# Chunks 4 and 5 of an mLSTM in 64x64 tiles, and FFN2 of the first group ahead of FFN1 of the third

## The chip, the cores and the metric

The kernel runs on one NeuronCore of a Trainium2 chip. The core has a matrix engine (TensorE, PE in the profile; its weight loads are PEld), three engines for elementwise work (VectorE or DVE, ScalarE or ACT, GpSimd or POOL), and a queue (SyncE, SP) that mostly issues DMA transfers; POOL issues some too. Each engine works through its own instructions in the order in which they were written, and waits on semaphores for the others. The metric is the device time of one execution in microseconds (us).

## The reference

An mLSTM cell runs over 4 batches, 8 heads and 768 time steps with 40 numbers per head; its output, as rows of 320, goes through a feed-forward network with a squared ReLU. Everything is in 32-bit floats; the two weight matrices arrive as 64-bit floats.

```python
for t in range(S):
    kt, vt, qt = (k[:, :, t], v[:, :, t], q[:, :, t])
    m_new = np.maximum(f_gate[:, :, t] + m, i_gate[:, :, t])
    f_stab = np.exp(f_gate[:, :, t] + m - m_new)
    i_stab = np.exp(i_gate[:, :, t] - m_new)
    m = m_new
    C = f_stab[:, :, None, None] * C + i_stab[:, :, None, None] * np.einsum('bhd,bhe->bhde', vt, kt)
    n = f_stab[:, :, None] * n + i_stab[:, :, None] * kt
    h_tilde = np.einsum('bhde,bhe->bhd', C, qt)
    denom = np.maximum(np.abs(np.einsum('bhd,bhd->bh', n, qt)[:, :, None]), 1.0)
    y[:, :, t] = h_tilde / denom / (1.0 + np.exp(-o_gate[:, :, t]))
x = y.transpose(0, 2, 1, 3).reshape(3072, 320)
out = np.maximum(x @ w_in, 0.0) ** 2 @ w_out        # w_in 320 x 2048, w_out 2048 x 320
```

## The kernel before

**Chunks and groups.** Time is cut into 24 chunks of 128 steps (`NT`), six per batch (`NB`). Within a chunk the recurrence becomes products of matrices: scores (keys by queries), scores times a matrix W of decays, that times the values (the numerators), and a state C carried to the next chunk of the batch. Two chunks make a group (`GT`), 12 groups in all; FFN1 and FFN2 work on a group's 256 rows. Chunks and groups are numbered from 0.

**Two forms of a chunk.** Chunks 0 to 5 (below `X_SQ`) use the whole 128x128 array: `transposes` turns keys and queries, `scores` multiplies them, `weigh` makes W with one exponential per head, `weighted` applies it, and `attend` computes `hi` (old state by queries, L622), `dC` (new state, L634) and `hp` (values by weighted scores, L645). `normalise` divides on DVE, `turn_rows` turns the rows of x for the FFN on PE (L848, L850), and ACT copies them out (L853).

Chunks from 6 on use 64x64 quarters of the array. `attend_begin` and `attend_end` hold two halves of the products into `numT`: `values_of_C` (old state, L708), `values_of_P` (values, L727), `new_C` (new state, L738). Between the halves stands one tiny DVE instruction (L700) that reads the last result of the first half, and the second half waits for it. The numerators come out turned. DVE transposes 32x32 squares of them (`tn`, L758); `store_num` writes them to memory, `load_num` reads them back in another order, `normalise_turned` divides, `store_rows` and `load_rows` take x through memory the same way, and `turn_squares` (L840) finishes the turning. `decays` (L488, L492) gives the old state's factors, which `scale_q` (L672) puts on the queries; `decay_C` scales the old state on POOL. From chunk 7 on (`KQ_SQ`) keys and queries are turned in the same manner (`pair_up`, `load_squares`, `turn_kq`), from chunk 8 on (`ROT`) the causal zeros are skipped too.

**Weights.** `Rounding` brings the 64-bit weights in 18 pieces: `fetch` loads one on SP (L210), `words` makes two conversions on ACT (L220, L222), `join` three instructions on DVE (L231 to L236) and one on POOL (L240), after which it fetches the next. Pieces 0 to 9 are `w_in`, 10 to 17 `w_out`.

**FFN.** Groups 0 and 1 have a plain FFN1 (`ffn1`, L874 and L885; `relu_half` and `square_half` on ACT), group 0 a plain FFN2 (`ffn2`, L911, 64 products). From group 2 (FFN1) and group 1 (FFN2) on, seven products of half-size blocks do the work of eight. FFN1 then is `ffn1_open`, `ffn1_rows` (64-row products, L1090) and `ffn1_close`, whose sums end on DVE at L1111; it needs sums of weights (`sums_of_win`) and of x (`sums_of_x`, on DVE for group 2, else on POOL). FFN2 is `ffn2_fast` in four steps (L965), with sums of weights (`sums_of_weights`, T0 to T2 and B12 in place) and of activations (`sums`, S1 to S4).

**Order.** It is written out by hand. After a set-up that ends at about 25 us, a first loop of eight passes (u) does chunks 2 to 5, two passes each, beside FFN1 of groups 0 and 1, while pieces of weights arrive. A second loop (n) runs over quarters of FFN work: four parts for FFN1 of group 2, four for FFN2 of group 0, then FFN2 of group g and FFN1 of group g + 2 in turn. Chunk 6 + n // 4 runs beside them: its scores and `weighted` in its first part, `attend_begin` and `attend_end` in its second, the next chunk's weighing and its own normalising in its third. Loads of keys and values (`load`) go out on SP below chunk 10 and on POOL from there. `NEXT` and `LAST` say how many pieces of weights are joined after each pass or part.

PSUM has eight banks. In the first loop three are for FFN1 (`ps_h`), two for others (`ps_o`) and three for attention (`ps_at`); in the second loop five and three. A product that wants a bank waits until the earlier result has been copied out of it.

Of the kernel before, what the change touches and what calls it, by code (L numbers as in the profile page):

```python
# [29 lines left out]
def kernel(  # L30
# [80 lines left out]
    bdm = conv.tile([P, PR, 2, D1], F32, bufs=1)  # L111
# [13 lines left out]
    def make_consts():  # L125
# [24 lines left out]
        nc.gpsimd.memset(bdm[:], 1.0)  # L150
        nc.gpsimd.memset(bdm[:DP, :, 1, :], 0.0)
        nc.gpsimd.memset(bdm[DP:, :, 0, :], 0.0)
# [30 lines left out]
    class Rounding:  # L183
# [41 lines left out]
        def join(self):  # L225
# [16 lines left out]
            if n != LENT - 1:  # L242
                self.fetch()
# [95 lines left out]
    KQ_SQ, X_SQ, ROT = 7, 6, 8  # L339
# [22 lines left out]
    def load_k(s):  # L362
        (dst, src), _, _ = load_parts(s)
        b, c = divmod(s, NB)
        src = src[b, :, c * P : (c + 1) * P, :].rearrange("h p d -> p h d")
        eng = nc.sync if s < 10 else nc.gpsimd
        eng.dma_start(dst[:, :PR], src[:, :PR])
        for n in range(2):
            eng.dma_start(dst[HALVES[n], PR:], src[HALVES[1 - n], PR:])

    def load_v(s):
# [3 lines left out]
        eng = nc.sync if s < 10 else nc.gpsimd  # L375
# [15 lines left out]
    def kqT(s):  # L391
        t = kqT_b[s % NKT]
        st[s]["kT"], st[s]["qT"] = t[:, 0], t[:, 1]
        return t
# [69 lines left out]

    def mask(s):
# [14 lines left out]
    def decays(s):  # L480

        if s % NB > 0:
            e = st[s]["eA"] = kq_b[2 + s % 2][:, 1].rearrange("p (j two) d -> p j (two d)", two=2)
# [10 lines left out]
    def weigh(s, masked=False, part=None, vw=True):  # L494
# [4 lines left out]
        if s < X_SQ and part != 1:  # L499
# [8 lines left out]
        for i in (range(len(A) if s < ROT else 0) if part is None else (part,)):  # L508
# [5 lines left out]
            if s < X_SQ:  # L514
# [84 lines left out]
    C_old = []  # L599

    def decay_old(s):
        if s + 1 < NB:
            Cd = st[s]["Cd"] = old.tile([P, PR, 2, D1], F32, name="Cd", bufs=1)
            nc.gpsimd.tensor_tensor(
                Cd[:].rearrange("p j i d -> p (j i) d"), C_old[(s - 1) % 2][:].rearrange("p j i d -> p (j i) d"),
# [3 lines left out]
    def attend(s):  # L609
# [41 lines left out]
        if c > 0:  # L651
            num = d["num"] = old.tile([P, H, D1], F32, name="num", bufs=1)
            nc.vector.tensor_tensor(
                num[:], hi[:], eA_T[:, b, c, :].unsqueeze(2).to_broadcast([P, H, D1]), op=ALU.mult,
# [3 lines left out]
        if c + 1 < NB:  # L658
            Cn = C_old[s % 2]
            if c == 0:  # L660
                nc.vector.tensor_tensor(Cn[:], dC[:], bdm[:], op=ALU.mult)
# [12 lines left out]
    def decay_C(s):  # L674
        if s % NB > 0:
            Cd = st[s]["Cd"] = attn.tile([P, PR, D1], F32, name="Cd", bufs=1)
            nc.gpsimd.tensor_tensor(
                Cd[:], C_b[(s - 1) % 2][:, : PR * D1].rearrange("p (j d) -> p j d", d=D1),
# [3 lines left out]
    LIVE = [slice(DP * i, DP * i + D) for i in range(2)]  # L682

    def attend_begin(s):
# [13 lines left out]
        else:  # L698
            end, spare = out[1][DP : DP + 1, P : P + 1], C_b[(s - 1) % 2][0:1, 4 * D1 : 4 * D1 + 1]
        nc.vector.tensor_scalar(spare, end, scalar1=0.0, scalar2=None, op0=ALU.mult)  # L700

    def values_of_C(s, rows, order=(0, 1)):
        d = st[s]
        C = C_b[(s - 1) % 2]
        for e in order:
            for m in order:
                i, j = rows[m], 2 * m + e
                nc.tensor.matmul(  # L708
                    d["numT"][m][HALVES[e], i, :], lhsT=C[LIVE[i], j * D1 : j * D1 + DP], rhs=d["eA"][LIVE[i], j, :],
# [33 lines left out]
    def attend_end(s):  # L743
# [11 lines left out]
        tn = attn.tile([P, P // SQ, PR, SQ], F32, name="tn", bufs=1)  # L755
        to = tn[:].rearrange("p m c r -> p c m r")
# [3 lines left out]
        if c + 1 < NB:  # L760
            Cn = C_b[s % 2][:, : PR * D1].rearrange("p (m x) -> p m x", m=2)
            for m in range(2):
                dC = d["out"][m][:, 2 * P : 2 * P + 2 * D1]
                if c > 0:
                    nc.vector.tensor_tensor(
                        Cn[:, m], dC, d["Cd"][:].rearrange("p (m e) d -> p m (e d)", m=2)[:, m], op=ALU.add,
# [5 lines left out]
    def store_num(s):  # L772
        nc.sync.dma_start(n_d[s], st[s]["tn"][:].rearrange("p m j r -> p (m j r)"))

    def load_num(s):
        N = st[s]["N"] = kq_b[s % 2][:, 1].rearrange("p h d -> p (h d)")
# [28 lines left out]
    def normalise(s):  # L805
        d = st[s]
        num = d["num"]
        if num is not d["hp"]:
            nc.vector.tensor_tensor(num[:], num[:], d["hp"][:], op=ALU.add)
# [96 lines left out]
    def ffn2(g, j, part):  # L906
        if part == 0:
            st["o_ps"] = ps_h.tile([P, W], F32, name="h_ps")[:, :DM]
        o_ps = st["o_ps"]
        for fb in range(part * NF // 2, (part + 1) * NF // 2):  # L910
            nc.tensor.matmul(  # L911
                o_ps, lhsT=st["g2", g][:, fb, j * P : (j + 1) * P], rhs=w_out[:, fb, :],
                start=(fb == 0), stop=(fb == NF - 1),
            )
        if part == 1:
            y = ffn.tile([P, DM], F32, name="y_sb", bufs=3)
            nc.scalar.copy(y[:], o_ps)
            t = g * GT + j
            nc.sync.dma_start(out[t * P : (t + 1) * P, :], y[:])

# [118 lines left out]
    def ffn1_begin(g):  # L1046
        new_g2(g)
        xT = st["xT", g]
        begun = st["begun"] = [
            (ps_h.tile([P, 4, P], F32, name="h_ps"), ffn.tile([P, 4, P], F32, name="r_sb", bufs=4)) for _ in range(2)  # L1050
        ]
        for q, (X, m1) in enumerate(begun):
            blocks(X, F11, xT[:, 0, 0, :], q, True)
            nc.scalar.copy(m1[:], X[:])
        for q, (X, m1) in enumerate(begun):
            blocks(X, F12, xT[:, 0, 1, :], q, False)

    def ffn1_open(g, q):
        if q == 0 and g > 2:
            new_g2(g)  # L1060
        xT, xs = st["xT", g], st["xs"]
        begun = st["begun"].pop(0) if g == 2 else None
        X = begun[0] if begun else ps_h.tile([P, 4, P], F32, name="h_ps")
        Y, V, Z = [ps_h.tile([P, 4, P], F32, name="h_ps") for _ in range(3)]
        st["f1"] = X, Y, V, Z
        m1 = begun[1] if begun else ffn.tile([P, 4, P], F32, name="r_sb", bufs=4)
        U2, U4 = [ffn.tile([P, 4, P], F32, name="r_sb", bufs=4) for _ in range(2)]
        st["U"] = U2, U4
        if not begun:
# [391 lines left out]
```

## Time and profile before

| | us |
|---|---|
| median of the three runs | 492.54 (490.52 to 492.83) |
| the profiled execution, in all | 491.22 |
| its span in the profile | 489.4 |
| PE busy | 481.7 |
| DVE busy | 341.8 |
| ACT busy | 240.4 |
| POOL busy | 215.3 |

The profile records one execution. For each instruction it gives its engine, the line of the program, its start and duration, and what released it when the engine had been idle before. A 32-bit product appears as two instructions (so "x16" is eight products), and a matmul's own duration overlaps the next one's; the chain of work shows what each group adds to the time. Rows of the chain are: start, length, engine and line, count. Rows of a timeline are: start, length, engine, line, operation, output<-input, shapes, count, and in brackets idle time before it and its releaser. Stage rows give, for a stretch, its length and each engine's busy time with the number of its instructions, the granted clock of TensorE, and the busy share of the DMA engines. Waits are: who, for whom, total, times, longest.

### The profile page before, as it was taken

What the parts mean: (1) busy time and instruction counts of PE and PEld (TensorE: products, weight loads), DVE (VectorE), ACT (ScalarE), POOL (GpSimd) and SP (SyncE); (2) the same over time, 40 slices, a digit from 0 to 9 for tenths busy, and PEclk for the clock granted to TensorE, in tenths of its full rate; (3) what the DMA queues carried; (4) which work ended last, traced back from release to release, by engine and by line L of the source; (5) the groups of instructions that cost most, each with busy time, mean ns of one, the idle gap of its engine ahead of it and who ended that gap; (6) DMA issues with size and microseconds to landing.
All of it is one profiled execution on the core that took longest, in us unless ns stands there. A gap on an engine that the chain in (4) does not pass through costs nothing.

```text
span 489.4 us, 15237 instructions
## 1 busy us (share of the span) xinstructions
PE 481.7 (98%) x6169; PEld 449.0 (92%) x6169; DVE 341.8 (70%) x704; ACT 240.4 (49%) x531; POOL 215.3 (44%) x322
## 2 busy tenths in 40 slices
PE   9999999999999999999999999999999999999997
PEld 4886788897799999999999999999999999999996
DVE  7799767888946856957966956857856956635441
ACT  4676996764522650942742941742942640513300
POOL 6455533432679178078179078078174040020000
PEclk9999999999999999999999999999999999999999
DMA  9999997745878579758759778658665612200000
GB/s 185 227 243 227 304 230 183 151 84 140 171 130 199 120 138 225 134 107 212 135 99 219 140 117 208 134 109 213 123 106 129 149 51 82 55 28 2 3 27 29
DMA packets 191096, 68.08 MB, mean 139 GB/s; under 512 B 158833, under 2 KB 180241, under 8 KB 191025
## 3 DMA queue, kind: packets, MB, share of 16 engines
q1 hardware_dynamic: 185280, 57.50, 55.1%
q0 software_dynamic: 5600, 9.50, 8.1%
q8 instruction: 49, 0.80, 0.7%
q14 instruction: 23, 0.18, 0.1%
q10 hardware_dynamic: 144, 0.10, 0.1%
HBM read 54.77 MB, written 18.01 MB: 149 GB/s over the span
## 4 chain that ended last, share of the span: by engine, by line
PE 87%; ACT 5%; SPq 4%; DMA 3%; issue 1%; DVE 0%; ACTq 0%
PE h_ps L965 35%; PE h_ps L1041 26%; PE h_ps L1090 8%; PE h_ps L911 4%; PE h_ps L874 3%; PE numT L727 3%; PE numT L708 2%; DMA lent_t<-in_moe_w_in_dram 1%; PE numT L738 1%; SPq L210 1%; PE tp L575 1%; PE h_ps L575 1%; SPq L1151 1%; ACT g_c L511 1%; DMA raw<-in_moe_w_in_dram 1%; DMA og<-in_o_gate_dram 1%
## 5 line engine op out<-in xcount | busy, mean ns | idle before, releaser
L475 POOL TENSOR_SCALAR_AFFINE_SELECT A_bc<-A_bc 64x512 f32<-64x512 f32 x32 | 22.5, 704 | 80.4 <-ACT kq L492 57.9
L965 PE MATMUL h_ps<-T,S 128*128 128x160 f32 x352 | 51.7, 300 | 0.6 <-ACT g_c L1107 0.6
L1071 ACT COPY r_sb<-h_ps 128x512 f32<-128x512 f32 x18 | 10.5, 585 | 84.2 <-PE h_ps L1041 84.2
L965 PEld LDWEIGHTS h_ps<-T,S 128*128 128x128 f32 x352 | 48.9, 190 | 1.1 <-ACT g_c L1107 0.9
L965 PE MATMUL h_ps<-w_out,g 128*128 128x160 f32 x336 | 49.2, 303 | 0.0
L981 DVE TENSOR_TENSOR y_sb<-y_sb,h_ps 128x160 f32<-128x160 f32 x44 | 14.1, 320 | 47.7 <-PE h_ps L965 47.6
L965 PEld LDWEIGHTS h_ps<-w_out,g 128*128 128x128 f32 x336 | 46.1, 190 | 1.3 <-issue 0.5
L1041 PE MATMUL h_ps<-xT,w_in 128*128 128x128 f32 x320 | 42.8, 278 | 0.0
L1041 PE MATMUL h_ps<-lent_t,w_in 128*128 128x128 f32 x320 | 42.2, 275 | 0.0
L1041 PEld LDWEIGHTS h_ps<-xT,w_in 128*128 128x128 f32 x320 | 38.9, 192 | 1.4 <-issue 1.0
L1090 PE MATMUL h_ps<-xT,w_in 64*64 64x128 f32 x960 | 39.1, 272 | 0.0
L1041 PEld LDWEIGHTS h_ps<-lent_t,w_in 128*128 128x128 f32 x320 | 38.9, 192 | 0.2 <-issue 0.2
L1041 PE MATMUL h_ps<-lent_t 128*128 128x128 f32 x320 | 39.0, 275 | 0.0
L1041 PEld LDWEIGHTS h_ps<-lent_t 128*128 128x128 f32 x320 | 37.3, 192 | 0.0
L505 ACT ACTIVATE A_bc<-A_bc,b_R 128x64 f32<-128x64 f32 (+1 forms) x128 | 35.7, 361 | 1.8 <-POOL A_bc L475 1.4
L1090 PEld LDWEIGHTS h_ps<-xT,w_in 64*64 64x64 f32 x960 | 34.8, 133 | 1.3
L379 POOL DMA_DIRECT2D va<-in_v_dram x56 | 34.2, 619 | 1.8 <-DMA kq_rows<-in_q_dram 1.3
L758 DVE STREAM_TRANSPOSE tn<-numT 128x256 f32<-128x256 f32 x36 | 14.0, 428 | 28.5 <-PE numT L708 19.2
L874 PE MATMUL h_ps<-xT,w_in 128*128 128x256 f32 x128 | 30.1, 385 | 1.6 <-ACT xT L853 1.2
L874 PEld LDWEIGHTS h_ps<-xT,w_in 128*128 128x128 f32 x128 | 23.4, 190 | 6.1 <-POOL w_in L240 1.6
L1033 POOL TENSOR_TENSOR lent_t<-xT 128x128 f32<-128x128 f32 (+1 forms) x18 | 14.6, 833 | 32.7 <-DVE xT L840 32.7
L965 PE MATMUL h_ps<-w_out,g_c 128*128 128x160 f32 x192 | 28.0, 302 | 0.0
(218 smaller groups left out, 1150.0 us busy)
## 6 DMA issues: line engine op xcount, KB each, us to landing
A_bc<-a_slots SPq DMA_DIRECT2D x32, 256.0 KB, 4.4
num_rows<-tn SPq DMA_DIRECT2D x18, 256.0 KB, 2.3
kq<-num_rows SPq DMA_DIRECT2D x72, 64.0 KB, 2.1
raw<-in_moe_w_out_dram SPq DMA_DIRECT2D x7, 640.0 KB, 5.4
kqT<-kq_rows SPq DMA_DIRECT2D x34, 128.0 KB, 3.3
og<-in_o_gate_dram SPq DMA_DIRECT2D x24, 160.0 KB, 4.9
out_dram<-y_sb SPq DMA_DIRECT2D x24, 160.0 KB, 3.1
raw<-in_moe_w_in_dram SPq DMA_DIRECT2D x7, 512.0 KB, 6.9
```

The source lines that it names most:

```text
L379: eng.dma_start(dst[HALVES[n], PR * (1 - late_keys) : PR * (2 - late_keys)], src[HALVES[late_keys], PR * m : PR * (m + 1)],)
L475: nc.gpsimd.affine_select(part, part, compare_op=ALU.is_ge, fill=-1e30, base=0, pattern=[[0, PR], [0, 2], [1, DP]], channel_multiplier=-1,)
L505: nc.scalar.activation(A[0][:, x, to], A[0][:, x, to], AF.Exp, bias=b_R[:, b, c, own, x : x + 1],)
L727: nc.tensor.matmul(d["numT"][m][HALVES[e], i, t0:], lhsT=va_w[s % NKQ][keys, at * D1 : at * D1 + DP], rhs=rhs, start=(s % NB == 0 and i == ...
L758: nc.vector.transpose(to[:, 2 * m : 2 * m + 2], d["numT"][m].rearrange("p c t -> p (c t)"))
L874: nc.tensor.matmul(hs[i][:, n, :], lhsT=w_in[:, a, fb * P : (fb + 1) * P], rhs=xT[:, :, a, :], start=(n == 0 and a == 0), stop=False,)
L911: nc.tensor.matmul(o_ps, lhsT=st["g2", g][:, fb, j * P : (j + 1) * P], rhs=w_out[:, fb, :], start=(fb == 0), stop=(fb == NF - 1),)
L965: nc.tensor.matmul(to, lhsT=lhsT[:, p], rhs=rhs[:, p, :], start=(start and p == 0), stop=(p == NPAIR - 1), skip_group_check=True,)
L981: add = lambda to, a, b: nc.vector.tensor_tensor(to, a, b, op=ALU.add)
L1033: sub = lambda to, a, b: eng.tensor_tensor(to, a, b, op=ALU.subtract)
L1041: nc.tensor.matmul(to[:, n, :], lhsT=lhsT[:, 4 * q + n, :], rhs=rhs, start=(start and n == 0), stop=True, skip_group_check=True,)
L1090: nc.tensor.matmul(to[cols, n, :], lhsT=w_in2[rows, 4 * q + n, cols], rhs=rhs, start=(start and n == 0), stop=True, skip_group_check=True,)
```

## The change

`X_SQ` goes from 6 to 4, so chunks 4 and 5 take the quarter form. Their `decays` and `scale_q` are new work in the first loop; their numerators and rows go through memory; their og gets the second ACT copy of `half_tanh`. Chunk 4's old state is still in the layout of the whole-tile form, so `values_of_C` picks its columns out of it. W for chunks 4 and 5 is masked after the exponential (`mask_W`) and not before. In u = 2 chunk 4's exponentials move ahead of a piece's `words`. The block mask `bdm` goes: two copies onto a zeroed tile take its place.

In the second loop FFN2 of group 0 is first and FFN1 of group 2 second; FFN2's products run in an order that needs the last piece of `w_out` only in the fourth part; `ffn1_begin`, a split opening for group 2, goes. The sums move to other parts: sums of weights 0, 1, 3, 2 to n = 3, 4, 9, 9 (they were 0, 1, 2, 3 at n = 5, 6, 7, 8), S1 and S2 of group 1 to n = 6 and 7 (both were at n = 6). Chunks 8 and 9 are loaded at n = 5 and 6 on POOL (they were loaded in u = 5 and u = 7 on SP), chunk 10 at n = 8; og for 8 and 9 comes at n = 3, `pair_up` for 8 and 9 at n = 0 and 2. Chunk 7's numerators are stored (n = 5) before chunk 6's rows are loaded back.

```diff
@@ set-up @@
-    bdm = conv.tile([P, PR, 2, D1], F32, bufs=1)
...
-        nc.gpsimd.memset(bdm[:], 1.0)
-        nc.gpsimd.memset(bdm[:DP, :, 1, :], 0.0)
-        nc.gpsimd.memset(bdm[DP:, :, 0, :], 0.0)
...
-    KQ_SQ, X_SQ, ROT = 7, 6, 8
+    KQ_SQ, X_SQ, ROT = 7, 4, 8
...
-        eng = nc.sync if s < 10 else nc.gpsimd
+        eng = nc.gpsimd
...
+    def mask_W(s):
+        nc.gpsimd.affine_select(
+            st[s]["W"], st[s]["W"], compare_op=ALU.is_ge, fill=0.0, base=0, pattern=[[0, H], [1, P]],
+            channel_multiplier=-1,
+        )
@@ decay_old, attend, values_of_C @@
+            if s >= X_SQ:
...
+                for i, rows in enumerate(HALVES):
+                    nc.gpsimd.tensor_tensor(
+                        Cd[rows], C_old[(s - 1) % 2][rows, :, i, :],
+                        st[s]["dec"][rows, i::2].unsqueeze(2).to_broadcast([DP, PR, D1]), op=ALU.mult,
+                    )
+                return
...
-            if c == 0:
-                nc.vector.tensor_tensor(Cn[:], dC[:], bdm[:], op=ALU.mult)
+            for i in range(2 if c == 0 else 0):
+                nc.vector.tensor_copy(Cn[HALVES[i], :, i, :], dC[HALVES[i], :, i, :])
...
+    def state(s):
+        return (C_b if s >= NB else C_flat)[s % 2]
...
+                at = (2 * j + i if s == X_SQ else j) * D1
@@ ffn2 @@
+    F2 = [(j, fb) for half in ((0, 8), (8, 14), (14, 16)) for j in range(GT) for fb in range(*half)]
+
+    def ffn2(step):
+        if step == 0:
+            st["o_ps"] = [ps_h.tile([P, W], F32, name="h_ps")[:, :DM] for _ in range(GT)]
+        for j, fb in F2[8 * step : 8 * step + 8]:
...
+        if step == 3:
+            for j, o_ps in enumerate(st["o_ps"]):
+                y = ffn.tile([P, DM], F32, name="y_sb", bufs=3)
+                nc.scalar.copy(y[:], o_ps)
+                nc.sync.dma_start(out[j * P : (j + 1) * P, :], y[:])
@@ first loop @@
-    WIN_SUMS = {5: 0, 6: 1, 7: 3}
+    WIN_SUMS = {5: (0, 1), 6: (3,)}
...
             if u == 2:
+                weigh(4, masked=True, vw=False)
+                decays(4)
                 rounding.words()
             weighted(s)
...
             if u == 2:
-                mask(s + 1)
                 rounding.join()
+                mask_W(4)
                 rounding.join()
-                weigh(s + 1, masked=True)
+                values(4)
                 rounding.words()
             else:
...
-                weigh(s + 1, masked=(u == 0), vw=(u > 0))
+                weigh(s + 1, masked=(u != 6), vw=(u == 6))
+                if u == 4:
+                    mask_W(5)
                 square_half()
+                if u > 0:
+                    scale_q(s)
...
-            attend(s)
+            if s < X_SQ:
+                attend(s)
+            else:
+                attend_begin(s)
+                attend_end(s)
+                store_num(s)
...
-            for r in {5: (8,), 7: (9,)}.get(u, ()):
-                load(r)
-            for r in {5: (7,), 7: (8,)}.get(u, ()):
-                pair_up(r)
+            if u == 5:
+                pair_up(7)
+            if u == 7:
+                load_A(7)
             if u > 4:
-                load_o(2 * s)
-                load_o(2 * s + 1)
+                load_num(s)
             transposes(s + 1, (True, True))
             rounding.words()
             ffn1(u // 4, u % 4)
             square_half()
+            if u == 5:
+                decays(5)
+            if u == 7:
+                normalise_turned(4)
+                store_rows(4)
+                rounding.fetch()
+                rounding.join()
...
+        if u == 6:
+            load_squares(7)
...
-    turn_rows(5)
-    load_squares(7)
@@ second loop @@
-    parts = [(1, 2, i) for i in range(4)] + [(2, 0, i) for i in range(4)]
-    for g in range(1, NG):
+    parts = []
+    for g in range(NG):
...
+        if n == 0:
+            turn_kq(7)
+            pair_up(8)
+            load_rows(4)
+            rounding.words()
+            rounding.join()
...
             do(store_num, s)
+            if n == 1:
+                normalise_turned(5)
+                store_rows(5)
+                turn_squares(4)
+            if n == 5:
+                load_rows(6)
             do(load_num, s)
+            if n == 1:
+                load_rows(5)
+                weigh(7, masked=True)
+                sums_of_win(2)
             do(load_squares, s + 2)
...
-        if 5 <= n < 8:
-            sums_of_weights(n - 5)
-        if n == 6:
-            sums(1, slice(0, NPAIR), (1, 2))
+        if n == 3:
+            load_o(8)
+            load_o(9)
+            sums_of_weights(0)
         if n == 8:
-            sums_of_weights(3)
             sums(1, slice(0, NPAIR), (3,))
         if n == 9:
+            sums_of_weights(3)
             sums(1, slice(0, NPAIR), (4,))
+            sums_of_weights(2)
...
-        if n == 0:
-            ffn1_begin(g)
-            sums_of_x(g)
-            sums_of_win(2)
...
+            if n == 6:
+                sums(1, slice(0, NPAIR), (1,))
+                turn_squares(6)
...
+            if n == 2:
+                pair_up(9)
+                turn_squares(5)
+                sums_of_x(2)
...
+        if n in (5, 6):
+            load(3 + n)
+            load_o(5 + n)
+        if n == 8:
+            load(10)
...
+        if n == 4:
+            sums_of_weights(1)
+        if n == 7:
+            sums(1, slice(0, NPAIR), (2,))
```

## The prediction, made before the changed kernel was run

> **What bounds the kernel now.** I read the page's busy shares first, then the busy time by stage, then the waits of PE, then the chain of work around the edited stages, and last the timelines of ACT and DVE there. Chunks are numbered from 0, as in the code, so the change concerns chunks 4 and 5; u counts the eight passes of the first loop, n the parts of the second.
>
> ```profile
> span 489.4 us, 15237 instructions
> PE 481.7 (98%) x6169; PEld 449.0 (92%) x6169; DVE 341.8 (70%) x704; ACT 240.4 (49%) x531; POOL 215.3 (44%) x322
> ```
> ```profile
> 59.00:91.06 32.06, 30.90 (x221) 25.51 (x217) 23.37 (x38) 27.01 (x55) 11.85 (x9) 1.00 0.93 196
> 91.06:130.09 39.03, 38.75 (x485) 32.25 (x488) 33.41 (x66) 23.42 (x51) 15.82 (x23) 1.00 0.60 124
> ```
> ```profile
> PE h_ps L874 <- ACT xT L853: 1.2, 1, 1.2
> ```
>
> From 60.56 us on TensorE pauses hardly at all (0.28 in the second stage), at a granted clock of 1.00. So this time is a sum of TensorE's work, and a change is worth the products it takes away, less the pauses it brings. The stage lines (length, then busy PE, PEld, DVE, ACT, POOL, clock, DMA share) show what stands close behind: ACT with 27.01 of 32.06 us in the stage of chunks 4 and 5, DVE with 33.41 of 39.03 us in the next. The one long wait of PE is for the copy of chunk 3's rows, behind a full ACT queue.
>
> ```profile
> 65.35 1.05 PE hi L622 x8
> 66.40 0.89 PE dC L634 x8
> 67.29 1.75 PE hp L645 x16
> ...
> 74.47 0.37 PE tp L848 x2
> 74.83 0.37 PE tp L850 x4
> ```
> ```profile
> 114.54 0.38 PE numT L708 x8
> 114.92 0.44 PE numT L727 x16
> 115.36 0.26 PE numT L738 x16
> ...
> 115.64 0.17 DVE kq L700
> ...
> 115.85 0.44 PE numT L738 x16
> 116.29 0.46 PE numT L727 x16
> 116.75 0.22 PE numT L708 x8
> ```
> ```profile
> 48.93 0.68 ACT L220 ACTIVATE mag<-raw 128x512 f32<-128x512 f32 x1 [4.27 <-DMA raw<-in_moe_w_in_dram]
> 50.08 2.43 ACT L511 ACTIVATE g_c<-A_bc,b_T 128x128 f32<-128x128 f32 x8
> ```
> ```profile
> 169.12 0.68 DVE L1111 TENSOR_TENSOR g<-r_sb,h_ps 128x512 f32<-128x512 f32 x1
> ```
>
> The first of these is chunk 4 in whole tiles, the second chunk 7 in quarters: the two prices that the change trades.
>
> **Part 1, chunk 4 in quarters.** Goes: hi, dC and hp, 1.05 + 0.89 + 1.75 = 3.69, and the turning of its rows, 0.37 + 0.37 = 0.74. Comes: chunk 7's row, 114.54 to 116.97 = 2.43, since chunk 4 too has a state before and after, works below ROT and has nothing between the halves. Gain 1.26 + 0.74 = 2.00.
>
> **Part 2, chunk 5.** Goes: 1.05 + 1.75 = 2.80 (no state follows) and 0.74. Comes: 0.38 + 0.44 in the first half, the wait for L700 (115.61 to 115.85, 0.24) with the refilling behind it (0.44 instead of the 0.21 of the same products at 155.30, so 0.23), then 0.22 + 0.46: 1.97. Gain 0.83 + 0.74 = 1.57.
>
> [...]
>
> **Part 3, ACT at u = 2.** The exponentials of chunk 4 (2.43) and its decays (2 of 0.62) go ahead of a weight piece's two conversions. ACT idles 4.27 us there, from 44.65 to 48.93, so they fit: 44.65 + 2.43 + 1.25 = 48.33. After it ACT no longer has the 2.43 at 50.08. The next piece (issued at 45.28) lands at 51.29, so ACT runs 52.52 - 51.3 = 1.2 us earlier through the relu, square and copies up to L853. Of PE's 1.16 us of wait I take 1.10 as gone; bounds 0 and 1.16.
>
> **Part 4, FFN2 of group 0 ahead of FFN1 of group 2.** The number of products is the same. Chunk 7's halves now stand around the 64-row products, as chunk 9's do at 152.50 (0.38, 0.44, 0.21, then 0.21, 0.46, 0.22 = 1.92), and not bare: 2.43 - 1.92 = 0.51. FFN1 of group 2 loses its split opening: 6.50 + 6.45 = 12.95 against 3.57 + 9.13 = 12.70 for group 3, 0.25. Gain 0.76, bounds 0 and 0.76.
>
> Gains: 2.00 + 1.57 + 1.10 + 0.76 = 5.43. The new clock, for what follows: chunk 6's scores (89.97 before) start at 89.97 - 4.67 = 85.3, FFN2 of group 0 at 86.4, chunk 6's halves at 86.4 + 4.5 = 90.9; with chunk 7's scores they take 1.48 + 0.88, to 93.3; the other 13.12 of FFN2 end at 106.4, the first part of FFN1 at 110.0 (3.57), chunk 7 with the 64-row products between its halves (1.92 + 1.77) at 113.7, its state on DVE (0.78 + 0.35) at 114.9.
>
> **Part 5, what DVE gets late.** S2 of group 1 was made at n = 6, far ahead; now it stands at n = 7 behind the closing sums of FFN1. In group 3 these ended at 169.72, 2.70 after PE had gone on to the scores at 167.02. With S2's 1.22 that is 3.92; PE wants S2 after scores (0.67) and half of a step (4.54 / 2), 2.94. So PE waits 1.0; bounds 0 and 1.5. The fourth sum of weights (1.48) moves from n = 8 to behind chunk 8's state at n = 9: state done 138.91, so 140.39, against 137.87 + 2.27 = 140.14 for the product that reads it: 0.3 with the semaphore; bounds 0 and 0.5. The other moved sums (weights 0, 1, 2, S1, S3, S4, the first two of w_in) stand behind work that PE does not want next.
>
> **Part 6, POOL.** Loads of chunks 8 and 9, seven issues each, move from SP to POOL and from u = 5, 7 to n = 5, 6: 14 x 0.62 = 8.7 us. They come behind Cd(8), which needs chunk 7's state (114.9). Then: Cd 0.5, load(8) 4.5, waiting for its last landing 2.4 to 5.8, vw 0.75, pair_up(10) 2.1, load(9) 4.5, load(10) 4.5, mask(9) 1.4, Cd(9) 0.5, load(11) 4.5, spreading 1.8, vw(9) 0.75, the sums of x for group 3 1.6. With 3.8 of waiting this ends at 146.2; PE wants them at 132.4 (end of chunk 8, 137.87 less 5.43) + 11.06 + 0.89 + 1.3 (part 5) = 145.7. I take 0.5; bounds 0 (landing in 2.4) and 2.5. DVE's weighting of chunk 9 waits behind vw(9), with the closing of FFN2 behind it.
>
> [...]
>
> **Costs set at nothing.** ACT gains 2.5 of decays and 0.94 of copies of og and loses two row copies of 0.48: from 64.3 it then runs without a gap until 79.4, and the tightest relu is 0.7 ahead of the bank that PE wants at u = 6; without that, each us is a us. SP: two chunks more of storing and loading (0.34 + 1.75 + 0.38 + 1.85, 4.3 each) take the place of the two loads (4.5 each); two og loads and their issues go to n = 3. Two waits stand in SP's queue: chunk 4's rows wait for its normalising (1.9 on DVE in u = 7), and behind them the last raw piece, which FFN2 reads at about 104.5; chunk 5's rows wait for its normalising, and behind them chunk 6's numerators (landing by 101, normalised from 101.8 on, when DVE is through with weights and chunk 7), chunk 5's rows, chunk 8's squares (wanted at 118) and decays (110). DVE: L700, tn, state and normalising (0.16 + 0.78 + 0.35 + 1.9) with scale and turn (0.7 + 0.55) are 4.4, as the old row (4.4 from 66.44). The x of chunk 5 must reach FFN1 of group 2: normalised by 96.4 (tn and state of chunk 6 to 94.5, then 1.9), stored in 3.5 (as at 109.66), loaded in 3.5 (as at 113.24) to 103.4, turned behind chunk 6's normalising and summed by 105.6; PE wants it 0.89 after 106.4, at 107.3: cover 1.7. The set-up (a second zeroing of 0.4 on POOL, three less, two copies for one product on DVE, 0.2 more) lies beside the first loads.
>
> **Sum.** -5.43 + 1.0 + 0.3 + 0.5 = -3.63. The profiled execution had 489.4 of span and 491.22 in all: 487.6. It lies 1.3 under the median of 492.54; between 487.6 and 488.9 I say 488.3.
>
> **Rivals.** (a) The gain is given back: the next piece lands late so the 1.10 stays, and POOL is 2.5 late: -5.43 + 1.10 + 1.3 + 2.5 = -0.5, 490.7. For it: POOL's chain has no slack; against: the landing at 51.29 is on record. (b) No new wait shows, since DVE is ahead at n = 7 and POOL's landings are short: -5.43, 485.8. Against it: the closing sums can't start before PE has finished the part. (c) Slower: the x of chunk 5 comes late to n = 4. Each us beyond the 1.7 of cover costs one; it decides from 5.3 us late. For it: at 130.87 the same load took 6.95, twice the 3.5. With both hops doubled it is loaded at 110.4 and summed at 112.1, a pause of 4.8; with that alone added, -3.63 + 4.8 = +1.2, 492.4. Against it: no POOL loads run at that time in the new order.
>
> **How the numbers follow.** Mine 0.45, (a) 0.25, (b) 0.12, (c) and what is like it 0.18. Half a per cent, 2.5 us, is about what a measurement can tell. Mine is beyond it nine times in ten, (b) always, (a) seldom: faster 0.55, same 0.27, slower 0.18. The range goes from (b), 485.8 less some scatter, to (c), 492.4 with the median's 1.3: 485.0 to 494.0; mine alone is 486.5 to 490.5.
>
> **What would show it.** No hi, hp or tp L848 after 60 us; quarters of 2.4 and 2.0 us for chunks 4 and 5; no wait of PE for L853; FFN2 of group 0 starting near 86; a wait of 1 us for DVE's S2 near 128; POOL without idle time from 115 to 146. I am wrong if PE waits between 100 and 110 for the sums of x, or in the first loop for relu.

## The result, and the profile after

Over twelve executions each, the changed kernel and the kernel before have the same median, 492.24 us (490.80 to 495.06 against 490.52 to 492.83): a ratio of 1.0006, 95% interval 0.9989 to 1.0024. I had forecast 488.3, 4.2 us under the median that I then knew. The profiled execution took 491.6, with this head of its page:

```profile
span 489.9 us, 15406 instructions
PE 477.5 (97%) x6229; PEld 445.9 (91%) x6229; DVE 343.4 (70%) x719; ACT 242.9 (50%) x534; POOL 228.3 (47%) x335
```

TensorE has 4.2 us less to do (481.7 before) and needs 0.5 more of span: its idle time went from 7.7 to 12.4 us. So the products were saved, and pauses took the time back. Where, the busy time by stage tells (length of the stretch, then busy PE, PEld, DVE, ACT, POOL, granted clock, DMA share, GB/s). After the change the stretches are: to the scores of chunk 6 and the start of FFN2; to the scores of chunk 8 (n = 8); to FFN1 of group 3 (n = 12); to its second block of products; the rest.

```profile
60.51:87.61 27.10, 26.22 (x273) 21.54 (x273) 20.81 (x41) 24.82 (x51) 12.31 (x7) 1.00 0.93 209
87.61:125.76 38.15, 38.15 (x480) 32.22 (x484) 30.89 (x69) 18.79 (x43) 18.48 (x24) 1.00 0.73 157
125.76:148.40 22.64, 19.21 (x265) 18.35 (x258) 17.31 (x26) 10.52 (x26) 20.55 (x31) 1.00 0.98 164
148.40:150.22 1.82, 1.05 (x10) 0.86 (x8) 1.47 (x4) 0.59 (x1) 1.77 (x4) 1.00 0.92 232
150.22:489.90 339.68, 335.94 (x4792) 328.66 (x4792) 222.86 (x479) 144.34 (x311) 143.92 (x223) 1.00 0.54 117
```

The kernel before, in the stretch that answers to the third (it runs 0.13 us into FFN1 of group 3, which starts there at 148.77):

```profile
130.02:148.90 18.88, 18.88 (x259) 18.47 (x259) 11.76 (x22) 4.58 (x15) 13.26 (x21) 1.00 0.82 145
```

Chunk 8's scores start at 125.76 instead of 130.02, 4.26 us sooner; that much of the 5.43 was made. In the third stretch PE idles 3.4 of 22.64 us where it had idled none, and another 0.8 in the fourth. From the second block of FFN1's products on, both kernels need 339.7 us. The same products of the third stretch also keep PE busy for 19.21 us instead of 18.75 (to 148.77). I put this down to the last product ahead of a pause, which overlaps no next one: the five instructions ahead of the longest pause, in the timeline below, took 0.95 us, 0.19 each, and the 27 behind it 3.94, 0.15 each. The waits of PE name three pauses for that stretch (us in total, times, longest):

```profile
PE h_ps L980 <- issue: 2.2, 1, 2.2
PE h_ps L980 <- DVE S L975: 1.2, 1, 1.2
...
PE h_ps L1056 <- POOL lent_t L1051: 0.8, 1, 0.8
PE h_ps L896 <- ACT xT L875: 0.7, 1, 0.7
```

The first three are 4.2 us and take back all but 0.06 of the 4.26; with the 0.46 more of busy time the span is 0.5 longer than before. The timeline of PE (start, duration, and in brackets the idle time ahead and who ended it) shows all three. In the longest, of the 16 instructions of a step of L980, five ran and then nothing for 2.24 us, though no semaphore was waited for ("issue"):

```profile
130.17 2.41 PE L980 MATMUL h_ps<-T,S 128*128 128x160 f32 x16 [1.19 <-DVE S L975]
...
134.92 0.95 PE L980 MATMUL h_ps<-w_out,g 128*128 128x160 f32 x5
138.11 3.94 PE L980 MATMUL h_ps<-w_out,g 128*128 128x160 f32 x27 [2.24 <-issue]
...
148.40 1.05 PE L1056 MATMUL h_ps<-xT,w_in 128*128 128x128 f32 x8
150.22 2.05 PE L1056 MATMUL h_ps<-lent_t 128*128 128x128 f32 x16 [0.77 <-POOL lent_t L1051]
```

POOL explains the wait of 0.77. After the change its timeline reads:

```profile
133.53 0.62 POOL L365 DMA_DIRECT2D kq<-in_k_dram  x1 [0.77 <-DMA kq<-in_k_dram]
134.60 0.62 POOL L375 DMA_DIRECT2D va<-in_v_dram  x1 [0.45 <-DMA kq<-in_k_dram]
135.51 0.62 POOL L375 DMA_DIRECT2D va<-in_v_dram  x1 [0.29 <-DMA va<-in_v_dram]
136.54 1.22 POOL L375 DMA_DIRECT2D va<-in_v_dram  x2 [0.41 <-DMA va<-in_v_dram]
137.77 2.29 POOL L478 TENSOR_SCALAR_AFFINE_SELECT A_bc<-A_bc 64x512 f32<-64x512 f32 x2
140.14 1.57 POOL L692 TENSOR_TENSOR Cd<-C,kq 128x164 f32<-128x164 f32 x1
...
149.72 0.45 POOL L1051 TENSOR_TENSOR lent_t<-lent_t,xT 128x128 f32<-128x128 f32 x1
```

and POOL's timeline of the kernel before, at the same step:

```profile
139.13 1.30 POOL L677 TENSOR_TENSOR Cd<-C,kq 128x164 f32<-128x164 f32 x1 [2.92 <-DVE C L765]
...
148.43 0.46 POOL L1036 TENSOR_TENSOR lent_t<-lent_t,xT 128x128 f32<-128x128 f32 x1
```

Before, POOL stood ready and made Cd of chunk 9 as soon as chunk 8's state came from DVE. Now that state is there at 136.1, but POOL is still issuing the load of chunk 10, with pauses of 0.3 to 0.8 us in which an issue waits for an earlier load to land (each time the load issued eight places before it, which had landed 0.28 us earlier), and then masks; Cd starts 4.0 us behind the state, and the sums of x, 10 us of work further on, end that much later.

### The profile page after: what moved, and what is told of

Its sections match the earlier page's. It is cut to its first block, busy times and chain, and to the rows that moved or that the text cites. A ratio compares the mean times of both kernels' runs of the same rounds, so it can differ in the third digit from the quotient of the medians.

```text
span 489.9 us, 15406 instructions
## 1 busy us (share of the span) xinstructions
PE 477.5 (97%) x6229; PEld 445.9 (91%) x6229; DVE 343.4 (70%) x719; ACT 242.9 (50%) x534; POOL 228.3 (47%) x335
## 4 chain that ended last, share of the span: by engine, by line
PE 80%; DVE 6%; ACT 5%; DMA 4%; issue 2%; SPq 1%; POOL 1%; DVEq 0%; POOLq 0%; ACTq 0%
PE h_ps L980 32%; PE h_ps L1056 22%; PE h_ps L1089 7%; PE h_ps L934 4%; PE numT L746 3%; PE h_ps L896 3%; PE numT L727 2%; DMA raw<-in_moe_w_out_dram 1%; DMA kqT<-kq_rows 1%; PE numT L757 1%; PE h_ps L579 1%; PE idle L1138 1%; DVE mag L231 1%; DMA num_rows<-tn 1%; PE h_ps L907 1%
## 5 line engine op out<-in xcount | busy, mean ns | idle before, releaser
L478 POOL TENSOR_SCALAR_AFFINE_SELECT A_bc<-A_bc 64x512 f32<-64x512 f32 x32 | 25.3, 791 | 86.4 <-ACT kq L496 63.2
L1070 ACT COPY r_sb<-h_ps 128x512 f32<-128x512 f32 x20 | 11.7, 586 | 84.6 <-PE h_ps L1056 84.6
L980 PE MATMUL h_ps<-T,S 128*128 128x160 f32 x352 | 51.8, 300 | 1.5 <-DVE S L975 1.2
L980 PE MATMUL h_ps<-w_out,g 128*128 128x160 f32 x336 | 49.4, 303 | 2.2 <-issue 2.2
L980 PEld LDWEIGHTS h_ps<-T,S 128*128 128x128 f32 x352 | 48.9, 190 | 2.2 <-ACT g_c L1116 1.4
L980 PEld LDWEIGHTS h_ps<-w_out,g 128*128 128x128 f32 x336 | 46.1, 190 | 3.8 <-issue 3.0
L375 POOL DMA_DIRECT2D va<-in_v_dram x64 | 39.2, 621 | 2.7 <-DMA kq_rows<-in_q_dram 0.9
L980 PE MATMUL h_ps<-w_out,g_c 128*128 128x160 f32 x192 | 28.0, 302 | 0.0
```

The lines of the kernel that those rows point to most:

```text
L375: eng.dma_start(dst[HALVES[n], PR * (1 - late_keys) : PR * (2 - late_keys)], src[HALVES[late_keys], PR * m : PR * (m + 1)],)
L478: nc.gpsimd.affine_select(part, part, compare_op=ALU.is_ge, fill=-1e30, base=0, pattern=[[0, PR], [0, 2], [1, DP]], channel_multiplier=-1,)
L980: nc.tensor.matmul(to, lhsT=lhsT[:, p], rhs=rhs[:, p, :], start=(start and p == 0), stop=(p == NPAIR - 1), skip_group_check=True,)
```

## The experiments

Each run below was timed against the kernel before. The changed kernel was not timed again beside them, so differences from it go by the two ratios.

**First set: who makes the pauses.** Counting the records of TensorE (products, weight loads and those of its sequencer) from the start, the pause of 2.24 us stands ahead of record 2754. The trace also has the transfers of a queue called instruction: 49 of 16 KB for 12,638 records, so one for about 256 instructions. They start every 200 to 350 records as a rule (35 of 48 steps); the one at 135.04 came 502 records behind the one at 123.11, and took 1.49 us. That gave Theory A: TensorE ran out of instructions because the DMA engines were crowded by late loads.

The first run moves the loads of chunks 8 and 9 ahead:

```diff
+        if n in (2, 3):
+            load(6 + n)
         if n in (5, 6):
-            load(3 + n)
             load_o(5 + n)
```

> The changed kernel, with the loads of chunks 8 and 9 (seven issues each, still on POOL) put back from n = 5 and 6 to n = 2 and 3, where POOL is idle. Theory A (late loads: they keep POOL's chain until 150.2, so PE waits 0.77 for the sums of x, and they crowd the DMA engines from 126 to 138 us, so the instructions that TensorE needs next are fetched late, the pause of 2.24 us at n = 9): both go, the wait of 1.2 for S2 stays; 2.2 + 0.8 = 3.0 us less than the changed kernel, about 2.9 less than the kernel before. Theory B (the pause comes from DVE writing the weights in place, L961, beside the products that read the same tile): the pause of 2.2 stays, 0.8 less at most. Theory C (the pause is an accident of one profiled execution): no pause here, and the time only 0.8 less.

Measured: 492.33 us against 492.28 of the kernel before, ratio 0.9988 (0.996 to 1.0015); the expected 3 us did not come. What held of Theory A is that the wait for POOL went. The waits of PE in this kernel (total, times, longest):

```profile
PE h_ps L980 <- DVE S L975: 1.8, 1, 1.8
PE h_ps L980 <- issue: 1.4, 1, 1.4
...
PE numT L727 <- issue: 1.0, 1, 1.0
...
PE h_ps L1056 <- issue: 0.9, 1, 0.9
```

The pause inside the product is there again, at the same instruction (not an accident of one execution, so Theory C falls), shorter; the wait for S2 grew to 1.8, since PE came 0.8 sooner (128.17 for 128.98) and DVE, busy without a gap, 0.2; and of two other pauses without a releaser, one of 0.85 at 154.91 is new and the one near 339 grew from 0.27 to 1.00. In 128 to 156 us the waits for S2 and the pauses sum to 4.1, as in the changed kernel. The loads alone were not the cause of the fetch's lateness: it started at 134.34, 4.3 us after PE had gone on at 130.00.

The second makes S2 sooner:

```diff
             if n == 6:
-                sums(1, slice(0, NPAIR), (1,))
+                sums(1, slice(0, NPAIR), (1, 2))
...
-        if n == 7:
-            sums(1, slice(0, NPAIR), (2,))
```

> The changed kernel, with S2 of group 1 made at n = 6 right behind S1, as in the kernel before. The wait of 1.2 us for DVE's S2 at n = 8 goes in any case. Theory A: POOL's chain to the sums of x ends at 150.2 whatever PE does, so what PE gains is waited for there or in the pause before: the pauses of n = 9 and n = 12 together grow from 3.0 to 4.2, and the time is the same as the changed kernel's within 0.4 us. Rival (each wait of PE is a cost of its own, as my prediction's sum has it): 1.2 us less than the changed kernel.

Measured: 494.22, ratio 1.0037 (1.0013 to 1.0062): slower than the kernel before, and by the ratios 1.5 us slower than the changed kernel, though these two intervals overlap. The wait for S2 went, and nothing was gained: PE now waits 3.13 us in one piece for POOL, whose chain ends at 150.33. Theory A's total of the two later pauses, 4.2, was 1.1 us too high: the pause at n = 9 is gone. The time did not stay the same, and the busy time by stage of this kernel shows a part of why (columns as above; the figure behind POOL's is the granted clock):

```profile
147.20:150.33 3.13, 0.00 (x1) 0.00 (x1) 1.46 (x4) 0.59 (x1) 3.06 (x6) 1.00 1.12 163
...
151.00:154.00 3.00, 3.00 (x18) 3.00 (x17) 2.51 (x9) 1.44 (x4) 3.00 (x7) 0.53 0.84 242
```

After the pause of 3.13 us the granted clock is 0.50 from 151.21 to 154.62, for 3.41 us in which TensorE is busy throughout; by an estimate, half of that, it costs 1.7. The pause near 342 (1.36 for the 0.27 at 339 in the changed kernel) adds 1.1 in this execution.

The third leaves everything in place and moves only the borders of the instruction blocks, by 64 products of one column where TensorE waits for the first loads:

```diff
-    idle(12)
+    idle(8)
+    dots(64)
```

> The changed kernel, with 64 one-column products (128 instructions of TensorE with their weight loads) in place of 4 of the 12 idle products at the start, where TensorE only waits. Nothing else differs, but each later instruction of TensorE stands 128 places further on, so the borders of the fetched blocks (16 KB, 256 instructions, by the records of the instruction queue) fall elsewhere: half a block earlier in the program. Theory A: the block that was wanted inside chunk 8's and 9's small products is now asked for before them; the pause of 2.24 us at n = 9 goes or shrinks below 1, and the wait for POOL's sums of x at n = 12 grows by as much, to 2 to 3 us; time the same within 0.5 us. Theory B (in-place write on DVE): the pause stays at 2.2. Theory C (accident): neither.

Measured: 493.0, ratio 1.0012 (0.9985 to 1.0039); the pauses are those of Theory A. The timeline of PE in this kernel:

```profile
135.69 2.44 PE L980 MATMUL h_ps<-w_out,g 128*128 128x160 f32 x16
138.32 2.44 PE L980 MATMUL h_ps<-w_out,g 128*128 128x160 f32 x16 [0.19 <-DVE w_out L961]
...
147.12 1.05 PE L1056 MATMUL h_ps<-xT,w_in 128*128 128x128 f32 x8
150.93 1.44 PE L1056 MATMUL h_ps<-lent_t 128*128 128x128 f32 x5 [2.76 <-POOL lent_t L1051]
```

No pause in the product that had one, with DVE's write in place (Theory B) still beside it; B falls. The wait for POOL grew from 0.77 to 2.76. So POOL's chain held PE to about 150 whatever PE lost between n = 8 and n = 12 (150.2, 150.3 and 150.9 in the three kernels): the fetch's pause of 2.24 us lay in front of a wait that would have been there anyway.

The fourth has both the earlier loads and the earlier S2 (the first two diffs).

> The changed kernel, with both: loads of chunks 8 and 9 at n = 2 and 3, and S2 at n = 6. Theory A: no pause at n = 8, 9 and 12; 1.2 + 2.2 + 0.8 = 4.2 us less than the changed kernel, about 4.1 less than the kernel before (ratio 0.992). Rival: something else is late next (ACT's relu, POOL's loads of chunk 10, DVE's weights): between 1.5 and 3 less.

Measured: 490.38, ratio 0.9953 (0.9928 to 0.9977). Faster than the kernel before by 1.9 us, and by the ratios 2.6 less than the changed kernel and not 4.2; the rival's range. Late next were DVE's weighting of chunk 8 (attend held up 0.5 to 0.7 at 132.1), POOL's sums of x (0.53) and a pause of 1.09 near 338. This execution also came to chunk 8's scores at 126.72, 0.96 us later than the changed kernel's, with 1.6 us of waits for pieces of `w_in` in the first loop (0.6 there).

**Second set: what was late next, and the first loop.** The wait for the copied rows at 60 us was to go by my part 3; it only fell to 0.68. One run brings the weight piece that ACT waits for ahead of the gate rows:

```diff
-        if u < 4:
-            load_o(4 + u)
         while rounding.done < NEXT[u]:
             rounding.step()
+        if u < 4:
+            load_o(4 + u)
```

> The changed kernel, with the gate rows og that the first loop fetches in each pass (160 KB) issued behind the pass's weight pieces instead of ahead of them. In the profiles so far ACT takes up the piece of u = 2 0.08 to 0.10 us after it has landed, and the copy that TensorE waits for comes 7.6 us after the landing in four of five. Theory (my part 3 failed because the piece's landing, not ACT's queue, sets that copy): the piece is 160 KB nearer, so it lands some 0.7 us sooner after its issue (6.6 instead of 7.35) and the wait of 0.68 at 59.83 goes; the whole time stays within 0.5 us of the changed kernel's, since POOL's chain still ends near 150.2. Rival (the DMA engines share the bytes out, the order counts little): landing 7.3 after the issue, wait as before.

Measured, on the timeline of ACT; first the changed kernel's:

```profile
52.43 0.81 ACT L216 ACTIVATE mag<-raw 128x640 f32<-128x640 f32 x1 [2.11 <-DMA raw<-in_moe_w_out_dram]
...
59.96 0.49 ACT L875 COPY xT<-tp 128x384 f32<-128x384 f32 x1
```

and the same of this run:

```profile
51.14 0.81 ACT L216 ACTIVATE mag<-raw 128x640 f32<-128x640 f32 x1 [0.41 <-DMA raw<-in_moe_w_out_dram]
...
58.73 0.49 ACT L875 COPY xT<-tp 128x384 f32<-128x384 f32 x1
```

The piece lands 6.39 us after its issue instead of 7.35, the copy follows 7.6 us behind the landing in both, and PE's wait of 0.68 is gone. That the order of issue brought the landing forward isn't shown: with the old order it came 6.53 to 7.35 us after the issue in seven profiled executions, and with the new order once more, in the run with all edits below, 7.34. As a whole it is no better: 493.27, ratio 1.0026 (1.0006 to 1.0047), by the ratios 1 us over the changed kernel and not within the 0.5 expected, with intervals that overlap. PE came sooner to n = 8 and waited there: 1.11 for S2, 1.97 in the product, 1.11 for POOL.

The next has the earlier loads, S1 and S2 at n = 5 (their calls at n = 6 and 7 go) and the spreading behind the sums of x; of its diff, what is new:

```diff
             if fast:
                 ffn1_rows(g, 0, True)
+            if n == 5:
+                sums(1, slice(0, NPAIR), (1,))
             do(attend_end, s)
+            if n == 5:
+                sums(1, slice(0, NPAIR), (2,))
...
-        if n in (9, 25):
+        if n in (12, 25):
             spread_slots(2 + n // 25)
```

> Loads of chunks 8 and 9 at n = 2 and 3 as in the run with both edits, S1 and S2 of group 1 made at n = 5 (S1 between the halves of chunk 7, where DVE idles 2.0 us, S2 behind the state), and the spreading of the next sequence's gates on POOL at n = 12 instead of n = 9, behind the sums of x. Theory: what was late next in the run with both edits was DVE's weighting of chunk 8 (TensorE held up 0.5 to 0.7 inside chunk 8's first half) and POOL's sums of x (0.53): both go, 1.2 us less than that run, 489.2. The pause of 1.1 us near 338, ahead of instruction 8896, which is 24 blocks of 256 behind the one at 2752, stays. Rival: POOL's next loads become late by the spreading (1.8), no gain.

Measured: 489.41, ratio 0.9946 (0.9921 to 0.9971); 489.2 had been expected. The timeline of PE in this kernel:

```profile
134.05 2.44 PE L980 MATMUL h_ps<-w_out,g 128*128 128x160 f32 x16
137.05 2.44 PE L980 MATMUL h_ps<-w_out,g 128*128 128x160 f32 x16 [0.56 <-DVE w_out L961]
...
145.84 1.05 PE L1056 MATMUL h_ps<-xT,w_in 128*128 128x128 f32 x8
146.74 1.50 PE L1056 MATMUL h_ps<-lent_t 128*128 128x128 f32 x12
```

FFN1 of group 3 starts at 145.84 instead of 148.40 and runs into no wait for POOL. Of the three pauses none is left; 0.56 for the fourth sum of weights has come out from behind them. The pause near 338 stays (1.24).

The same with the 64 small products at the start (the third diff):

> The kernel of the run with sums sooner, with the 64 one-column products at the start in place of 4 idle ones, so that the borders of the instruction blocks fall 128 instructions earlier in the program. Theory (fetch of instructions): the pause near 338 goes, as in the shifted run, 1.1 us less than the run with sums sooner; no pause at n = 9. Rival: the pause near 338 has another cause (state of the chunk on DVE) and stays.

Measured: 488.65, ratio 0.9941 (0.9915 to 0.9966). The pause near 338 is gone; one of 0.42 came at 118.17. Against the run without the shift the medians differ by 0.8, less than the intervals of the two can tell apart; the trace of one execution, not the time, carries the point.

All edits together, the gate rows behind the pieces among them:

> All: loads of chunks 8 and 9 at n = 2 and 3, S1 and S2 at n = 5, spreading at n = 12, shifted instructions, and og behind the weight pieces. Theory: 0.6 less than the run with shifted instructions by the wait of TensorE for the copied rows at 60, now that nothing later takes it back; 487.5 to 488 us, a ratio of 0.990 to the kernel before. Rival: the first loop's landings scatter by 1 us from execution to execution and hide it.

Measured: 488.98, ratio 0.9942 (0.9918 to 0.9967): no gain on the last. In its profiled execution the piece landed 7.34 us after its issue and PE still waited 0.5 for the copied rows, which fits the rival, landings that scatter. It has a pause of 1.76 us at 172.69 instead, in the timeline of PE:

```profile
172.29 0.40 PE L727 MATMUL numT<-kq,C 40*64 40x128 f32 x8
174.45 1.85 PE L980 MATMUL h_ps<-w_out,g_c 128*128 128x160 f32 x8 [1.76 <-issue]
```

**Third set: the borders in the kernel before.** Three runs of the kernel before, one execution each, with 32, 64 and 96 one-column products at the start (diff as above):

> The kernel before, with 32 one-column products (64 instructions) in place of 2 idle ones at the start. Theory (blocks of 256 instructions): pauses of TensorE with no engine or DMA as releaser appear only at instruction counts that leave 194 (within 3) on division by 256, as 2242, 2754, 4034 and 8898 did in the changed kernels; one or two of 0.3 to 2 us over the span, or none if no border falls ahead of a chunk's small products. Rival: such pauses stand at other counts, so blocks are not their cause.

> The kernel before, with 64 one-column products (128 instructions) in place of 4 idle ones. As for 32; across the three shifts of the kernel before, at least one has such a pause, and each at 194 (within 3) on division by 256.

> The kernel before, with 96 one-column products (192 instructions) in place of 6 idle ones. As for 32; across the three shifts of the kernel before, at least one has such a pause, and each at 194 (within 3) on division by 256.

Every pause of 0.25 us or more that no engine or DMA ended, behind the first 26 us of the thirteen profiled executions, with the count of records ahead of it, is in this table. Left out is one of 0.32 ahead of FFN2 (L934, record 1412 in the changed kernel), which is in all of the changed kernels; it leaves 132 on division by 256 there and 250 in the shifted kernel, so it is no border, and its cause is open.

| kernel | pause at us (length): record | records modulo 256 |
|---|---|---|
| before | none | |
| before, shifted by 64 | 266.43 (0.37): 6591 | 191 |
| before, shifted by 128 | 338.33 (0.78): 8894 | 190 |
| before, shifted by 192 | 230.19 (0.56): 5567 | 191 |
| changed | 135.87 (2.24): 2754; 339.15 (0.27): 8898 | 194; 194 |
| loads early | 135.69 (1.40): 2752; 154.91 (0.85): 3264; 339.61 (1.00): 8896 | 192; 192; 192 |
| S2 early | 341.84 (1.36): 8896 | 192 |
| shifted | none | |
| loads and S2 | 337.06 (1.09): 8896 | 192 |
| piece first | 134.77 (1.97): 2754; 337.76 (0.68): 8898 | 194; 194 |
| sums sooner | 153.37 (0.39): 3265; 335.94 (1.24): 8897 | 193; 193 |
| and shifted | 118.17 (0.42): 2242 | 194 |
| all | 117.04 (0.31): 2242; 172.69 (1.76): 4034 | 194; 194 |

All 17 leave 190 to 194 (190 is one short of the 191 that I had allowed; a few records can be missing from a trace). The transfers say that these are borders of blocks, and that the pause is the wait for the block: with each transfer of 16 KB set beside the border that it serves (the first beside the one near record 449, the next 256 further on), none of the 627 borders in the thirteen executions is passed earlier than 1.24 us behind the end of its transfer, and the 17 pauses end 1.24 to 1.60 us behind it. In the kernel before, the tightest border has 2.06. The pause ahead of L934 ends 3.7 to 10.2 us behind the last transfer. The same kernel, shifted by less than a block, had other pauses at other places, in one execution each.

## Why the prediction was wrong

The step that failed is part 6, POOL, at 0.5 us with bounds 0 and 2.5. It measured 3.0: 2.24 + 0.77 in the changed kernel, where the pause for instructions took the first part of POOL's lateness, and, with that pause out of the way, 2.76 and 3.13 in single waits. I had the order of POOL's work right and its end at 146.2; it ended at 150.2. Of these 4.0 us (the terms add to 4.2), chunk 7's state was 1.1 later than I had it (116.0 for 114.9), the load of chunk 10 took 6.4 instead of 4.5 because its issues waited for landings (an issue itself took 0.62 as priced: 617 to 647 ns in the 64 of L375, 617 to 644 in the 56 of L379 in the kernel before), the masking 2.3 instead of 1.4, Cd 1.57 instead of 0.5, though the row of the kernel before at 139.13 already has 1.30 for it; the wait for chunk 8's load was 0.8 shorter. I priced these instructions and loads as they ran in calmer stretches, and then put 14 more transfers into this one. With loads early, POOL's chain ends at 147.18 instead of 150.17, 3.0 us sooner, and with S2 early too the kernel gets faster; that is shown. Why the masking took 2.3 is not.

Part 3 failed as well: of the 1.10 us expected, 0.05 came. The kernel before, copy and wait:

```profile
60.00 0.51 ACT L853 COPY xT<-tp 128x384 f32<-128x384 f32 x1
...
60.56 3.72 PE L874 MATMUL h_ps<-xT,w_in 128*128 128x256 f32 x16 [1.16 <-ACT xT L853]
```

and the wait of the changed kernel, whose copy at 59.96 stands above:

```profile
60.51 3.72 PE L896 MATMUL h_ps<-xT,w_in 128*128 128x256 f32 x16 [0.68 <-ACT xT L875]
```

From -3.63 in the sum to +0.5 in the span are 4.1 us; these two terms are 3.5 of them. The rest is the pause of 0.32 ahead of FFN2 and the 0.46 of products around pauses, less 0.2 of small terms.

- **Parts 1 and 2, quarters:** right. 2.43 and 1.98 us, as priced (2.43 and 1.97).
- **Part 3, ACT at u = 2:** wrong. PE's wait shrank by 0.48, but only because PE itself reached the rows 0.42 later (57.92 for 57.50, 0.24 of it in a wait for a piece of `w_in` at 53.64 that the kernel before had not); the copy came 0.04 sooner. ACT was free and waited 2.11 us for the piece, which landed at 52.35 and not at 51.29. I took a landing time from one execution; in the seven profiled executions of changed kernels with this order of issue it lay between 51.48 and 53.98 us, and in the three shifted ones of the kernel before between 52.15 and 52.59. The landing sets the copy: in eight of the nine changed kernels the copy follows 7.6 to 7.7 us behind it (8.3 in the shifted one).
- **Part 4, FFN2 first:** right. From the start of FFN2 (before: of FFN1) to chunk 8's scores, 39.03 us became 38.15, 0.88 for the 0.76; a pause of 0.32 just ahead of FFN2, which I had not counted, takes from it.
- **Part 5, DVE late:** S2 1.2 for my 1.0, right. The fourth sum of weights, at 0.3, showed nothing behind the other pause, and 0.19 to 0.56 without it: right.
- **Costs set at nothing:** PE waited for no relu in the first loop, and the x of chunk 5 landed at 104.8, in time for FFN1 at 107.5 (rival (c) did not happen). That PE was 0.42 late at 57.92 says that the first loop was not quite free of cost.
- **Rivals:** (a), POOL 2.5 late and the 1.10 kept, gave 490.7; the execution took 491.6. It was the case that came, and its text names both causes, POOL at 3.0 for its 2.5 and the 1.10 kept but for 0.05. I gave it 0.25.

What no step had is the pause at the block border. In this kernel it cost nothing of its own, as the shifted run shows, since it lay ahead of POOL's wait; with loads early, where POOL no longer holds PE, 1.40 us of it is lost.

Why the fetch at 135.04 was so late isn't settled. If a fetch is asked for about a block ahead, as the steps of the others suggest (their transfers start 239 records ahead of the border that they serve, by the median of the changed kernel, and 240 in the kernel before), this one belongs to the border some 256 records back, at about 2498, which PE reached just after its wait for S2 ended at 130.17; from there the next 256 records, the small products of chunks 8 and 9, were issued in 5.5 us. In the runs in which PE came to that border sooner (S2 early, loads and S2), the fetch started at 128.94 and 129.40 and nothing stopped. Whether the transfers of 129 to 137 us or the wait itself held it back was not told apart.

## What to carry to other kernels

When transfers move to an engine's queue, follow that queue to the next thing TensorE needs from it, and price the issues in the stretch where they will stand, with the waits for landings; POOL's busy share (44% before, 47% after) did not tell that it was no longer ready when its input came. A wait that is removed ahead of another engine's chain buys nothing until that chain is shortened, and one long wait can cost more than two short ones (3.13 us here, with a clock of 0.50 for 3.41 us behind it). With 64 to 192 small instructions of TensorE put in at the start, the pauses at its block borders (0.3 to 2.2 us) came and went far behind them, in one execution each: look for pauses that nothing ended before taking a small difference for the edit's own.

## What the runs showed of the hardware

TensorE stopped where its next block of 256 instructions wasn't there: 0.27 to 2.24 us, at 17 borders in eleven of thirteen profiled executions, and it went on 1.24 to 1.60 us behind the end of the block's transfer. The last two transfers ahead of the end of the pause at 135.87 us (changed kernel) had started 502 records apart, and TensorE went on 1.58 us behind the end of the second.

Three long pauses had a lower clock with them. From 0.9 us behind the end of a pause of 3.13 us (S2 early), 0.5 ahead of the end of one of 2.76 (shifted) and 0.7 behind one of 1.76 (all edits), the granted clock was 0.50 for 3.41 us each time; after 2.24 in the changed kernel and 1.97 with the piece first it stayed at 1.00. So the length of the pause alone did not decide it; what did is not shown. Over whole executions it shows as a mean clock of 0.997 or less: 12 of 64 of the kernel before (2.3 us longer by the medians). Of the kernels whose profile has PE waiting 0.77 us or more for POOL, the changed one has it in 7 of 12, S2 early in 10 of 12, shifted in 8 of 12, the piece first in 6 of 10; of the others, loads early and loads and S2 in 1 of 12 each, sums sooner in none of 8, the same shifted in 4 of 12, all edits in 3 of 10. So the lower clock goes with the wait for POOL. It does not account for the changed kernel's scatter: its seven executions at a lower clock are 0.7 us longer by the medians, and loads early scatters as widely (489.68 to 493.98) at the full clock.
